# Attention and two mixtures of experts on one core: batch 0's attention in one segment, weight conversion spread, the second stage's first operands made earlier

## Chip, cores and metric

The kernel runs on one core of a Trainium2 chip. The metric is the device time of one execution in microseconds (us), smaller being better. Three runs of the kernel before took 1521.54, 1523.45 and 1525.31 us (median 1523.45).

## What is computed

Three stages, each fed by the one before. All results must have float32 accuracy.

```
attention:  4 batches, 8 heads, 576 tokens, 64 per head; block-causal mask in blocks of 64;
            softmax with row maximum; out = attn @ v         -> x (2304 tokens x 512)
first MoE:  x = (sigmoid(x @ w_gate) * (x @ w_val)) @ w_out  (512 -> 1536 -> 512)
second MoE: p = probs / (sum(probs) + 1e-9)
            out = sum over 4 experts e of p[:, e] * (relu(x @ w1[e]) @ w2[e])  (512 -> 1024 -> 512)
```

`w_gate`, `w_val` and `w_out` arrive as 64-bit floats.

## The kernel before

**Number format.** Large products are done as three fast matmuls on float32r pairs: each operand is split into a high and a low part (one copy and one subtraction, `split_sb` L101, `split3` L732). The left layers of both MoEs use a seven-product Winograd form (products 1, 5, 2, 6, 7, 4, 3), so that sums of operand blocks are made beforehand (`winograd_left` L577, `sums` L814).

**Attention** (`attn_items` L127). Work goes by pairs of heads, four pairs per batch. A pair's queries are five tiles t = 0 to 4 (the last has 64 tokens, with both heads in one tile). Per tile: scores into a PSUM bank (`s_mm` L269), mask by memset, row maximum on VectorE, exp on ScalarE with its sum, normalisation on GpSimd (`norm` L330), transposes of the weights on TensorE and copies out of PSUM (`p_tr` L361), then the product with v (`pv_both` L394), which writes its result to DRAM (`xd`, L418). Batches 1 to 3 are segments "F" with split operands. Batch 0 is done natively in float32, in two segments: "A" does tiles 0 and 1 of all four pairs against the first 256 keys, "B" then does tiles 2 to 4 of all four pairs and loads and transposes q's remaining and all of k's chunks again. In A the scores rotate through five PSUM banks (`bank` L296: two `s` banks and the first MoE's `c1`, `c2`, `lo`), in B and F through the two `s` banks. A score bank is free again when its exp has read it. The tiles that F needs (`klz`, `q4`) share space with A's and B's, so they are made when batch 0's items end (`f_tiles` L935), and F items that need them before are held (`attn_next` L946).

**Conversion.** 12 blocks of gate and value weights are turned from 64 to 32 bits, summed and split (`conv_items` L514: two loads of 512 KB; bit work on VectorE with one ScalarE pass; four subtractions, and most of the splitting, on GpSimd) and written back to DRAM as 1.8 MB per block (`wcd`, L543). Every pass of the first MoE loads them again (`w1_load` L549). Raw tiles have 3 buffers.

**First MoE.** Four passes p of 576 tokens (one batch each) by 12 blocks f. `x1_prep` (L610) needs all of that batch's attention. Pass 0 also converts `w_out` (`wo_get` L556). The second layer (`l2_1` L689) of a pair of blocks is merged with the next pair's first layer.

**Order.** `_merge` (L37) interleaves two item lists by their costs. Batch 0's attention (up to place 1.05) is merged with the first NC0 = 7 conversions. The other five follow in pass 0, half a block per f (L987). Later attention is pulled in by `attn_to` (L961). A scheduler then orders each engine's instructions at compile time with a model of time. It takes the order written here as a priority, and an instruction whose tile has no free buffer waits. All DMAs are issued by SyncE (SP), in order. Each engine runs its own queue in order.

**Second MoE.** Three passes of 768 tokens by 16 blocks q of 256 columns (`l1_items` L835, `l2_items` L886), q and q+1 in a step. `x_prep` (L743) makes a pass's seven split left operands. For pass 0 its items are emitted in the first MoE's last pass (f = 5 to 9). The weights of q (`w_load` L785, `w_prep` L793) are in the pool `p2`, which is allocated when the first MoE's pool is released (L1017), so the first two blocks and the probabilities are loaded and split there, between the two MoEs (L1020 to L1031). Each block has two tiles, `w1p` (three right operands) and `w1q` (four), two buffers each.

Of the kernel before, what the change touches and what calls it, by code (L numbers as in the profile page):

```python
# [18 lines left out]
NC0 = 7  # L19
# [8 lines left out]
PTB = 3  # L28
EARLY = True
HB = 14  # L30
PRE0, PRE1 = 0.4, 0.9
# [24 lines left out]
def attention_moe_moe_kernel(  # L56
# [70 lines left out]
    def attn_items(segs):  # L127
# [3 lines left out]

# [3 lines left out]
        QTS = {"A": range(2), "B": range(2, 5), "F": range(5)}  # L135
        KTS = {"A": range(2), "B": range(5), "F": range(5)}
# [10 lines left out]
        def load(g, nm, src, c0, c1):  # L147
            _, b, pr, seg = pairs[g]
            if nat_of(g):
                if nm == "k" and seg == "A":  # L150
                    t = attn.tile([P, S], F32, tag="kl", name="kn", bufs=2)
                    t = t[:, :2 * P].rearrange("p (c h d) -> p c h d", c=2, h=2)
                elif nm == "k" and pr % 2:
# [92 lines left out]
        order = {"A": 0, "B": 0, "F": 0}  # L246
# [6 lines left out]
        def pt_late(i):  # L253
            return not nat_of(seq[i][0]) and (seq[i][2] == 4 or ring[i] % (PT_BUFS + PT2_BUFS) >= PT_BUFS)
# [14 lines left out]
        def s_mm(i):  # L269
# [26 lines left out]
            def bank():  # L296
                if seg == "A":
# [47 lines left out]
        def pt_tile(g, h):  # L345

            i = 0 if nat_of(g) else 2 * (g - first)
            x = (i + h) % PTB
# [71 lines left out]
        def prep_list(g):  # L420
            seg = pairs[g][3]
            r = [(False, 0.0, lambda: prep_alloc(g))]
            for nm, cs in (("q", QTS[seg]), ("k", KTS[seg])):
                for part in ([c for c in cs if c < 2], [c for c in cs if c >= 2]):
                    if part:
                        r.append((seg == "F" and nm == "k", 110.0 * len(part), lambda nm=nm, part=part: prep_tr(g, nm, part)))
            if seg == "F":
                r.append((True, 0.0, lambda: prep_q4(g)))
# [28 lines left out]
        def step_tr(s):  # L457
            if 0 <= s - LT < n:
                i = s - LT
                g, hs, t = seq[i]  # L460
                items.append((g, tr_late(s - LT), 110.0 * (t + 1) * len(hs), lambda: p_tr(i)))

        def step_s(s):
            if s < n:
                g, hs, t = seq[s]
                items.append((g, pt_late(s), 2 * 0.42 * P * (t + 1) * len(hs) + 10, lambda: s_mm(s)))
# [255 lines left out]
    if True:  # L722
# [20 lines left out]
        def x_prep(p):  # L743

            r = []
            d = {}

            def load(kt):
                if kt == 0:
                    d["x"] = p2r.tile([P, NKT, TP], F32, tag="xr", name="xr")  # L750
                nc.sync.dma_start(out=d["x"][:, kt], in_=x2_d[kt][:, p * TP:(p + 1) * TP])

            def a(t, k):
                return d["x"][:, k * KH:(k + 1) * KH, t * TH:(t + 1) * TH]

            def s(which):
                if which == 1:
                    d["s"] = p2r.tile([P, KH, TH], F32, tag="xsa", name="xs")
                    nc.gpsimd.tensor_tensor(out=d["s"], in0=a(1, 0), in1=a(1, 1), op=ALU.add)
                elif which == 2:  # L760
                    nc.gpsimd.tensor_tensor(out=d["s"], in0=d["s"], in1=a(0, 0), op=ALU.subtract)
                elif which == 4:
                    nc.gpsimd.tensor_tensor(out=d["s"], in0=a(0, 1), in1=d["s"], op=ALU.subtract)
                else:
                    d["s3"] = p2r.tile([P, KH, TH], F32, tag="xsb", name="xs")
                    nc.gpsimd.tensor_tensor(out=d["s3"], in0=a(0, 0), in1=a(1, 0), op=ALU.subtract)

            def part(m, src):
                t = xc[m] = p2r.tile([P, 2, KH, TH], F32R, tag=f"xc{m}", name=f"xc{m}")
                split3(t[:, 0], t[:, 1], src())  # L770

            for kt in range(NKT):
                r.append((0.0, lambda kt=kt: load(kt)))
            for f in (lambda: part(1, lambda: a(0, 0)), lambda: s(1), lambda: part(5, lambda: d["s"]),
                      lambda: part(2, lambda: a(0, 1)), lambda: s(2), lambda: part(6, lambda: d["s"]),
                      lambda: s(3), lambda: part(7, lambda: d["s3"]), lambda: part(4, lambda: a(1, 1)),
                      lambda: s(4), lambda: part(3, lambda: d["s"])):
                r.append((0.0, f))
            return r
# [3 lines left out]
        WOP = {1: ("p", 0), 2: ("p", 1), 3: ("p", 2), 5: ("q", 0), 6: ("q", 1), 7: ("q", 2), 4: ("q", 3)}  # L783

        def w_load(q):  # L785
            e, fo = q // QPE, (q % QPE) * QF
            r1 = p2.tile([P, NKT, QF], F32, tag="wr1", name="wr1", bufs=2)
            nc.sync.dma_start(out=r1, in_=w1[e, :, fo:fo + QF].rearrange("(c p) f -> p c f", p=P))
            r2 = p2.tile([P, 2, DM], F32, tag="wr2", name="wr2", bufs=2)
            nc.sync.dma_start(out=r2, in_=w2[e, fo:fo + QF, :].rearrange("(a p) d -> p a d", p=P))  # L790
            wq["r", q] = (r1, r2)

        def w_prep(q):  # L793
# [8 lines left out]

            def own():
                r1, d["r2"] = wq.pop(("r", q))
                d["r1"] = r1.rearrange("p (h k) (a f) -> p h k a f", h=2, a=2)
                t = wq[q, "p"] = p2.tile([P, 2, 3, QF], F32R, tag="w1p", name="w1p", bufs=2)
                src = r1.rearrange("p k (a f) -> p k a f", a=2)[:, :, 0, :]
                split3(t[:, 0, 0:2].rearrange("p j (k f) -> p (j k) f", f=P),
                       t[:, 1, 0:2].rearrange("p j (k f) -> p (j k) f", f=P), src)
                split3(v(t[:, 0, 2]), v(t[:, 1, 2]), b(1, 1))  # L810

            def sums(n):
                if n == 0:
                    d["t"] = p2.tile([P, 4, QF], F32, tag="wt", name="wt", bufs=2)  # L814
# [4 lines left out]
            def mixed():  # L819
                t = wq[q, "q"] = p2.tile([P, 2, 4, QF], F32R, tag="w1q", name="w1q", bufs=2)  # L820
                split3(t[:, 0], t[:, 1], d["t"])

            def second():
                t = wq[q, "2"] = p2.tile([P, 2, 2, DM], F32R, tag="w2", name="w2", bufs=3)
                split3(t[:, 0], t[:, 1], d["r2"], "a", "p")

            r.append((0.0, lambda: own()))
            r += [(0.0, lambda n=n: sums(n)) for n in range(4)]
            r.append((0.0, mixed))
            r.append((0.0, second))  # L830
            return r

# [53 lines left out]
        def l2_items(p, q0):  # L886
# [201 lines left out]
```

## Time and profile before

| | |
|---|---|
| profiled execution, its time | 1523.15 us |
| its span | 1521.4 us (1.75 us lie outside) |
| median of the three runs | 1523.45 us |
| TensorE (PE) matmul busy | 1457.4 us, 96% |
| VectorE (DVE) / ScalarE (ACT) / GpSimd (POOL) busy | 62% / 54% / 35% |
| mean granted TensorE clock | 0.97 of full |
| batch 0's attention | to 125 us |
| first MoE | about 134 to 746 us |
| second MoE | 751 to 1518 us |

An engine's busy time is the union of its instructions. Matmul ends are modelled, so a busy PE may still have gaps inside. The clock is either 2.4 GHz (1.0) or 1.2 GHz (0.5). A value in between is a mean over the stretch. A wait row names the instruction that waited and what ended its wait.

### The profile page before, as it was taken

What the parts mean: (1) busy time and instruction counts of PE and PEld (TensorE: products, weight loads), DVE (VectorE), ACT (ScalarE), POOL (GpSimd) and SP (SyncE); (2) the same over time, 40 slices, a digit from 0 to 9 for tenths busy, and PEclk for the clock granted to TensorE, in tenths of its full rate; (3) what the DMA queues carried; (4) which work ended last, traced back from release to release, by engine and by line L of the source; (5) the groups of instructions that cost most, each with busy time, mean ns of one, the idle gap of its engine ahead of it and who ended that gap; (6) DMA issues with size and microseconds to landing.
All of it is one profiled execution on the core that took longest, in us unless ns stands there. A gap on an engine that the chain in (4) does not pass through costs nothing.

```text
span 1521.4 us, 24168 instructions
## 1 busy us (share of the span) xinstructions
PE 1457.4 (96%) x8392; PEld 1272.3 (84%) x8392; DVE 939.6 (62%) x2044; ACT 821.2 (54%) x2010; POOL 534.1 (35%) x583
## 2 busy tenths in 40 slices
PE   6877999999999999999899999999999999999998
PEld 3335788888889889999788989889898998989897
DVE  5668889887665675665665445665445475454543
ACT  5558888888875565555444433444343453343431
POOL 7685556542210110110243333363322443224320
PEclk8677999999999999999999999999999999999999
DMA  8887899887646888797422221142212123122201
GB/s 231 245 267 252 296 294 289 263 291 226 181 153 209 276 281 263 256 329 261 150 70 70 83 70 56 56 155 81 70 56 68 60 81 111 56 70 69 71 28 42
DMA packets 179242, 244.89 MB, mean 161 GB/s; under 512 B 75441, under 2 KB 124593, under 8 KB 179121
## 3 DMA queue, kind: packets, MB, share of 16 engines
q1 hardware_dynamic: 179120, 243.35, 49.6%
q8 instruction: 67, 1.10, 0.3%
q14 instruction: 55, 0.44, 0.1%
HBM read 200.84 MB, written 42.47 MB: 160 GB/s over the span
## 4 chain that ended last, share of the span: by engine, by line
PE 84%; DVE 4%; DMA 3%; ACT 3%; POOL 3%; issue 2%; SPq 1%; POOLq 0%; ACTq 0%; DVEq 0%
PE c L96 35%; PE o L96 28%; PE lo L96 7%; PE s L96 4%; PE obank L96 3%; PE tbank L369 2%; PE s L282 1%; PE t L96 1%; PE tbank L197 1%; DMA raw<-in_moe_w_gate_dram 1%; POOL wt L817 1%; ACT pt L313 1%; PE tbank L388 1%; POOL pt L341 0%; DVE nm L311 0%
## 5 line engine op out<-in xcount | busy, mean ns | idle before, releaser
L96 PE MATMUL o<-w,hb 128*128 128x512 f32 x1728 | 450.0, 395 | 2.2 <-ACT hb L864 1.0
L96 PEld LDWEIGHTS o<-w,hb 128*128 128x128 f32 x1728 | 321.9, 188 | 58.3 <-ACT hb L864 1.4
L96 PE MATMUL c<-xc,w1q 128*128 128x384 f32 x1152 | 240.9, 339 | 1.7 <-ACT w1q L735 1.4
L817 POOL TENSOR_TENSOR wt<-wr 128x256 f32<-128x256 f32 x96 | 72.2, 773 | 470.3 <-DMA wr<-in_moe_w_dram 470.3
L96 PEld LDWEIGHTS c<-xc,w1q 128*128 128x128 f32 x1152 | 207.4, 188 | 16.6 <-ACT w1q L735 2.1
L865 DVE SCALAR_TENSOR_TENSOR hb<-c,hb 128x384 fp32r<-128x384 f32 x192 | 119.4, 642 | 142.4 <-ACT hb L864 142.2
L96 PE MATMUL c<-xc,w1p 128*128 128x384 f32 x864 | 188.7, 342 | 5.9 <-ACT w1p L735 5.9
L864 ACT ACTIVATE hb<-c 128x384 fp32r<-128x384 f32 x192 | 94.7, 514 | 171.1 <-PE c L96 143.3
L96 PE MATMUL lo<-g,wo 128*128 128x288 f32 x1008 | 172.6, 302 | 3.3 <-DVE x L707 1.4
L855 ACT ACTIVATE snap<-c 128x384 f32<-128x384 f32 x144 | 69.7, 491 | 195.3 <-PE c L96 189.9
L96 PEld LDWEIGHTS c<-xc,w1p 128*128 128x128 f32 x864 | 158.4, 191 | 15.1 <-ACT w1p L735 6.4
L898 DVE SCALAR_TENSOR_TENSOR acc<-o,pr_t,acc 128x512 f32<-128x512 f32 x126 | 90.7, 747 | 129.5 <-PE o L96 129.5
L96 PEld LDWEIGHTS lo<-g,wo 128*128 128x128 f32 x1008 | 145.1, 190 | 8.4 <-DVE x L707 2.8
L341 POOL TENSOR_SCALAR pt<-pt,nm 128x384 f32<-128x384 f32 (+4 forms) x140 | 93.8, 676 | 141.8 <-DVE nm L338 100.1
L738 POOL TENSOR_TENSOR w<-wr,w 128x1024 fp32r<-128x1024 f32 x48 | 119.7, 2499 | 50.7 <-ACT w L735 50.7
L862 DVE TENSOR_TENSOR c<-c,snap 128x384 f32<-128x384 f32 x144 | 75.6, 552 | 51.6 <-ACT snap L855 47.2
L96 PE MATMUL c<-xc,wa 128*128 128x288 f32 x540 | 88.1, 302 | 4.0 <-ACT xc L108 1.9
L707 DVE TENSOR_TENSOR x<-lo,x 128x288 f32<-128x288 f32 x140 | 63.4, 453 | 34.8 <-PE lo L96 34.2
L96 PE MATMUL c<-xc,wc 128*128 128x288 f32 x504 | 82.7, 299 | 1.1 <-ACT snap L647 1.0
L96 PEld LDWEIGHTS c<-xc,wa 128*128 128x128 f32 x540 | 77.1, 190 | 8.0 <-ACT xc L108 2.2
L651 DVE TENSOR_TENSOR c<-c,snap 128x288 f32<-128x288 f32 x120 | 54.4, 453 | 45.5 <-PE c L96 31.0
L647 ACT ACTIVATE snap<-c 128x288 f32<-128x288 f32 x126 | 51.4, 408 | 57.1 <-PE c L96 56.8
(139 smaller groups left out, 2507.9 us busy)
## 6 DMA issues: line engine op xcount, KB each, us to landing
wr<-in_moe_w_dram SPq DMA_DIRECT2D x96, 512.0 KB, 3.4
wa<-wcd SPq DMA_DIRECT2D x48, 512.0 KB, 4.4
wb<-wcd SPq DMA_DIRECT2D x48, 512.0 KB, 5.0
wc<-wcd SPq DMA_DIRECT2D x48, 512.0 KB, 4.5
wo<-wod SPq DMA_DIRECT2D x36, 512.0 KB, 5.5
wd<-wcd SPq DMA_DIRECT2D x48, 256.0 KB, 4.3
raw<-in_moe_w_gate_dram SPq DMA_DIRECT2D x12, 512.0 KB, 5.6
raw<-in_moe_w_val_dram SPq DMA_DIRECT2D x12, 512.0 KB, 5.6
```

The source lines that it names most:

```text
L96: ins = nc.tensor.matmul(out=out, lhsT=lhsT, rhs=rhs, start=start, stop=stop, skip_group_check=skip)
L341: nc.gpsimd.tensor_scalar(out=p, in0=p, scalar1=nm[:, 2 + x:3 + x], scalar2=1.0, op0=ALU.mult, op1=ALU.mult)
L647: nc.scalar.activation(out=t, in_=d["c1"][:, :TH1], func=AF.Copy)
L651: nc.vector.tensor_tensor(out=c, in0=d["c2"][:, :TH1], in1=d[n], op=ALU.add)
L707: nc.vector.tensor_tensor(out=x2[t, dm], in0=ps, in1=x2[t, dm], op=ALU.add)
L738: (nc.vector if eng_lo == "v" else nc.gpsimd).tensor_tensor(out=lo, in0=src, in1=hi.bitcast(F32), op=ALU.subtract)
L817: nc.gpsimd.tensor_tensor(out=v(t[:, n]), in0=x, in1=y, op=ALU.subtract)
L855: nc.scalar.activation(out=t, in_=d["c1"][:, :TH], func=AF.Copy)
L862: nc.vector.tensor_tensor(out=c, in0=d[tag][:, :TH], in1=d[n], op=ALU.add)
L864: nc.scalar.activation(out=t[:, 0], in_=c, func=AF.Relu)
L865: nc.vector.scalar_tensor_tensor(out=t[:, 1], in0=c, scalar=0.0, in1=t[:, 0].bitcast(F32), op0=ALU.max, op1=ALU.subtract)
L898: nc.vector.scalar_tensor_tensor(out=acc[tt, t], in0=ps, scalar=pr_t[:, ti, e:e + 1], in1=acc[tt, t], op0=ALU.mult, op1=ALU.add)
```

## The change

1. Batch 0 is one segment "N": per pair all five query tiles and all keys, loaded and transposed once. All its scores rotate through five banks. Its exp tiles use a ring of four (`pt` and `pt2`), tile 4 one `pt4` buffer, the transposed weights three `pTb` buffers. The F tiles are made at the start, and nothing is held any more.
2. The first 12% of batch 0's attention are emitted ahead of any conversion. NC0 is 5. The other seven blocks are spread evenly over f = 0 to 9 of pass 0.
3. `x_prep` uses `winograd_left` with tiles of 128x384 (8 loads, 8 GpSimd sums and 14 splits per pass, in place of 4, 4 and 7 of twice the size).
4. The second MoE's `w1` operands become tiles of two products each, `w1g` (a, b, c; five buffers over all blocks) and one `w1d` buffer. They, the raw `wr1`, `wt` (one buffer) and the probabilities move to the pool `p2r`, which exists once attention has ended. `x_prep(0)`, the loads and splits of blocks 0 and 1 (less the last two splits of block 1) and the probabilities are spread over f = 2 to 11 of the first MoE's last pass. `w2` is loaded and split apart (`w2_load`, `w2_prep`), its first two blocks after the first MoE.

```diff
-NC0 = 7
+NC0 = 5
+A00 = 0.12
+W1B = 5
...
-        QTS = {"A": range(2), "B": range(2, 5), "F": range(5)}
-        KTS = {"A": range(2), "B": range(5), "F": range(5)}
+        QTS = KTS = {"N": range(5), "F": range(5)}
...
             if t == 4:
-                if nat_of(g):
-                    return attn.tile([P, S], F32, tag="kl", name="pt4", bufs=2)
                 return pt2.tile([P, S], F32, tag="pt4", name="pt4")
-            if pairs[g][3] == "A":
-                if ring[i] % (PT_BUFS + 1) == PT_BUFS:
-                    return attn.tile([P, 1280], F32, tag="pTb0", name="ptx")
-            elif pt_late(i):
+            if ring[i] % (PT_BUFS + PT2_BUFS) >= PT_BUFS:
...
             def bank():
-                if seg == "A":
+                if native:
...
-            i = 0 if nat_of(g) else 2 * (g - first)
-            x = (i + h) % PTB
+            x = (2 * g + h) % PTB
...
+            def load(kk, t, h):
+                a = p2r.tile([P, TH], F32, tag="xr", name="xr", bufs=4)
+                o = p * TP + t * TH
+                nc.sync.dma_start(out=a, in_=x2_d[h * KH + kk][:, o:o + TH])
+                return a
+            return winograd_left(p2r, xc, load, TH)
...
+        def w2_load(q):
...
+        def w2_prep(q):
+            t = wq[q, "2"] = p2.tile([P, 2, 2, DM], F32R, tag="w2", name="w2", bufs=3)
+            split3(t[:, 0], t[:, 1], wq.pop(("r2", q)), "a", "p")
...
+            def pair(k, src):
+                t = wq[q, k] = p2r.tile([P, 2, 2, QF], F32R, tag="w1g", name="w1g", bufs=W1B)
+                split3(t[:, 0], t[:, 1], src)
...
+            def last():
+                t = wq[q, "d"] = p2r.tile([P, 2, 1, QF], F32R, tag="w1d", name="w1d")
+                split3(v(t[:, 0, 0]), v(t[:, 1, 0]), b(1, 1))
+            r.append((0.0, own))
+            r += [(0.0, lambda n=n: sums(n)) for n in range(2)]
+            r.append((0.0, lambda: pair("b", d["t"][:, 0:2])))
+            r += [(0.0, lambda n=n: sums(n)) for n in range(2, 4)]
+            r.append((0.0, lambda: pair("c", d["t"][:, 2:4])))
+            r.append((0.0, last))
...
-        a0 += [(queue[i][2], attn_next) for i in range(len(queue)) if place[i] < A1[0]]
+        attn_to(A00)
+        a0 = [(queue[i][2], attn_next) for i in range(pos[0], len(queue)) if place[i] < A1[0]]
...
-                pre = x_prep(0)
-                pre0 = list(pre)
+                wp = [w_prep(0), w_prep(1)]
+                pre = x_prep(0) + [(0.0, lambda: (w_load(0), w_load(1), p_prep()))] + wp[0] + wp[1][:-2]
...
-                    if p == 0 and NC0 + f // 2 < NF:
-                        c = cs[NC0 + f // 2]
-                        side += [x for _, x in (c[:len(c) // 2] if f % 2 == 0 else c[len(c) // 2:])]
-                    if p == NP1 - 1 and f >= 5:
-                        n = len(pre) * (f - 4) // 5 - len(pre) * (f - 5) // 5 if f < 10 else 0
-                        for _ in range(n):
-                            side.append(pre0.pop(0)[1])
+                    if p == 0:
+                        c = sum(cs[NC0:], [])
+                        side += [x for _, x in c[len(c) * f // (NF - 2):len(c) * (f + 1) // (NF - 2)]]
+                    if p == NP1 - 1 and f >= 2:
+                        side += [x for _, x in pre[len(pre) * (f - 2) // (NF - 2):len(pre) * (f - 1) // (NF - 2)]]
...
-        w_load(0)
-        w_load(1)
-        run(w_prep(0))
-        run(w_prep(1))
...
+        for q in (0, 1):
+            w2_load(q)
+        prev = [(0.0, lambda q=q: w2_prep(q)) for q in (0, 1)]
...
+                if (p, q0) == (0, 0):
+                    side += wp[1][-2:]
```

## Rows read from the trace of the kernel before

**Rows 1.** The page: TensorE's busy time, and its granted clock in 40 slices.
```profile
PE 1457.4 (96%) x8392; PEld 1272.3 (84%) x8392; DVE 939.6 (62%) x2044; ACT 821.2 (54%) x2010; POOL 534.1 (35%) x583
...
PEclk8677999999999999999999999999999999999999
```
**Rows 2.** Busy time by stretch: stretch, length, busy (instructions) per engine, clock, DMA, GB/s.
```profile
0.00:126.00 126.00, 95.17 (x400) 47.56 (x400) 81.86 (x213) 73.74 (x205) 93.61 (x121) 0.78 0.83 260
42.00:126.00 84.00, 66.19 (x282) 32.27 (x281) 58.47 (x145) 50.21 (x138) 65.13 (x78) 0.76 0.84 272
62.00:82.00 20.00, 16.53 (x88) 7.95 (x88) 14.48 (x37) 12.24 (x38) 18.47 (x23) 1.00 0.83 249
...
134.00:342.00 208.00, 198.69 (x1393) 168.39 (x1391) 180.45 (x503) 179.40 (x524) 111.14 (x139) 0.98 0.86 278
342.00:500.00 158.00, 156.98 (x1132) 137.15 (x1132) 101.45 (x311) 115.83 (x346) 28.25 (x51) 1.00 0.65 199
640.00:746.00 106.00, 104.73 (x782) 103.83 (x781) 64.37 (x153) 56.08 (x159) 4.13 (x2) 1.00 0.73 251
```
**Rows 3.** SP's timeline: stores of batch 0's results (xd0a from A, xd0b from B).
```profile
41.06 0.54 SPq L418 DMA_DIRECT2D xd0a<-xr  x1
...
69.30 0.45 SPq L418 DMA_DIRECT2D xd0b<-xr  x1
...
125.39 0.52 SPq L418 DMA_DIRECT2D xd0b<-xr  x1
```
**Rows 4.** Waits from 42 to 126 us: total us, times, longest.
```profile
PEld tbank L369 <- POOL pt L341: 10.2, 7, 3.7
...
PEld s L282 <- ACT pt L313: 7.4, 5, 1.9
```
**Rows 5.** Conversion: GpSimd on tile wt to 320 us; groups by line, whole run.
```profile
sum 320.00, DVE 0.00 ACT 0.00 POOL 92.34; mean DVE 0.00 ACT 0.00 POOL 46.17
...
L110 POOL TENSOR_TENSOR wd<-raw,wd 128x256 fp32r<-128x256 f32 x12 | 9.9, 829 | 6.2 <-ACT wd L108 6.2
...
L489 DVE SCALAR_TENSOR_TENSOR raw<-raw 128x512 int32<-128x512 int32 x36 | 28.2, 782 | 0.3
L487 DVE SCALAR_TENSOR_TENSOR raw<-raw 128x512 int32<-128x512 int32 x36 | 28.1, 781 | 1.2 <-ACT raw L485 0.8
...
L486 DVE TENSOR_SCALAR raw<-raw 128x512 int32<-128x512 int32 x36 | 18.1, 503 | 11.7 <-DMA raw<-in_moe_w_gate_dram 10.5 <-DMA raw<-in_moe_w_out_dram 0.6 <-POOL wb L110 0.6
```
**Rows 6.** DMA from 134 to 342 us; SP's stores of converted blocks (a block's wd).
```profile
DMA packets 46141, 57.85 MB, mean 278 GB/s; under 512 B 27170, under 2 KB 34338, under 8 KB 46115
...
107.99 0.73 SPq L543 DMA_DIRECT2D wcd<-wd  x1
...
L543 SPq DMA_DIRECT2D wcd<-wd x12: 319/329/732, 18.1 to 305.5; - x12
```
**Rows 7.** VectorE groups by line, first from 134 to 342, then 342 to 500 us.
```profile
L651 DVE TENSOR_TENSOR c<-c,snap 128x288 f32<-128x288 f32 x36 | 16.2, 449 | 3.5 <-PE c L96 2.6 <-ACT snap L647 0.4
...
L661 DVE SCALAR_TENSOR_TENSOR r<-t,r 128x288 f32<-128x288 f32 x24 | 14.7, 611 | 0.9 <-ACT t L660 0.8
...
L651 DVE TENSOR_TENSOR c<-c,snap 128x288 f32<-128x288 f32 x33 | 15.0, 455 | 17.0 <-PE c L96 10.8 <-ACT snap L647 6.0
L661 DVE SCALAR_TENSOR_TENSOR r<-t,r 128x288 f32<-128x288 f32 x22 | 11.0, 502 | 3.6 <-ACT t L660 3.5
```
**Rows 8.** Between the MoEs (timeline); then second MoE and its middle pass by stretch.
```profile
746.43 0.41 SPq L788 DMA_DIRECT2D wr<-in_moe_w_dram  x1
...
751.24 6.13 PE L96 MATMUL c<-xc,w1p 128*128 128x384 f32 x18 [5.95 <-ACT w1p L735]
...
751.20:1517.50 766.30, 762.36 (x3744) 682.10 (x3744) 412.86 (x644) 308.19 (x541) 273.59 (x246) 1.00 0.22 73
1004.54:1256.96 252.42, 252.42 (x1250) 226.66 (x1249) 138.87 (x216) 104.74 (x183) 94.30 (x84) 1.00 0.24 79
```
**Rows 9.** Busy time by stretch: where the early x_prep items sit.
```profile
526.00:540.00 14.00, 11.50 (x68) 10.45 (x67) 8.25 (x17) 7.14 (x18) 1.81 (x1) 0.84 0.95 342
```

More of the change, by code (lines that the diff above doesn't have):

```diff
@@ L149, in load @@
             if nat_of(g):
[L150 to L153, printed above, removed]
+                if nm == "k" and pr % 2:
                     t = attn.tile([P, 5 * P], F32, tag="tk", name="kn", bufs=3)
@@ L425, in prep_list @@
                     if part:
-                        r.append((seg == "F" and nm == "k", 110.0 * len(part), lambda nm=nm, part=part: prep_tr(g, nm, part)))
+                        r.append((False, 110.0 * len(part), lambda nm=nm, part=part: prep_tr(g, nm, part)))
             if seg == "F":
-                r.append((True, 0.0, lambda: prep_q4(g)))
+                r.append((False, 0.0, lambda: prep_q4(g)))
             return [(g, *x) for x in r]
@@ L460, in step_tr @@
                 g, hs, t = seq[i]
-                items.append((g, tr_late(s - LT), 110.0 * (t + 1) * len(hs), lambda: p_tr(i)))
+                items.append((g, False, 110.0 * (t + 1) * len(hs), lambda: p_tr(i)))
         def step_s(s):
@@ L465, in step_s @@
                 g, hs, t = seq[s]
-                items.append((g, pt_late(s), 2 * 0.42 * P * (t + 1) * len(hs) + 10, lambda: s_mm(s)))
+                items.append((g, False, 2 * 0.42 * P * (t + 1) * len(hs) + 10, lambda: s_mm(s)))
         def step_norm(s):
@@ L743, in x_prep @@
         def x_prep(p):
[L745 to L778, printed above, removed]
@@ L817, in sums, with p_prep @@
                 nc.gpsimd.tensor_tensor(out=v(t[:, n]), in0=x, in1=y, op=ALU.subtract)
[L819 to L830, printed above, removed]
-            return r
+            def last():
[7 more added lines that the diff above has]
+            r.append((0.0, last))
+            return r
+        prs = {}
+        def p_prep():
+            pr_t = prs["t"] = p2r.tile([P, NTT, E], F32, name="pr_t")
+            ps_t = p2r.tile([P, NTT], F32, name="ps_t")
+            nc.sync.dma_start(out=pr_t, in_=probs.rearrange("(t p) e -> p t e", p=P))
+            nc.vector.tensor_reduce(out=ps_t, in_=pr_t, axis=AX.X, op=ALU.add)
+            nc.vector.tensor_scalar(out=ps_t, in0=ps_t, scalar1=1e-9, scalar2=None, op0=ALU.add)
+            nc.vector.reciprocal(out=ps_t, in_=ps_t)
+            for e in range(E):
+                nc.vector.tensor_tensor(out=pr_t[:, :, e], in0=pr_t[:, :, e], in1=ps_t, op=ALU.mult)
         hb = {}
@@ L921, in l2_items @@
             return r
-        a0 = [it[2:] for it in attn_items([(0, "A")])]
-        queue = attn_items([(0, "B"), (1, "F"), (2, "F"), (3, "F")])
+        queue = attn_items([(0, "N"), (1, "F"), (2, "F"), (3, "F")])
         ends = [max(i for i, it in enumerate(queue) if it[0] == x) for x in range(4)]
@@ L932, in attention_moe_moe_kernel @@
         pos = [0]
-        held = []
-        def f_tiles():
-            for x in range(3):
-                t = (attn if x < 2 else pt2).tile([P, S], F32R, tag="kl" if x < 2 else "kl2", name=f"klz{x}", bufs=2 if x < 2 else 1)
-                nc.gpsimd.memset(t[64:128].bitcast(F32), 0.0)
-                klz.append(t)
-            for x in range(2):
-                q4.append(pt2.tile([P, P], F32R, name=f"q4{x}"))
-                nc.gpsimd.tensor_scalar(out=q4[x], in0=ident, scalar1=0.0, scalar2=0.0, op0=ALU.mult, op1=ALU.mult)
-        def attn_next():
-            x, late, _, fn = queue[pos[0]]
-            if pos[0] > ends[0] and not klz:
-                f_tiles()
-                while held:
-                    held.pop(0)()
-            if not klz and x > 0 and (late or held):
-                held.append(fn)
-            else:
-                fn()
+        for x in range(3):
+            t = (attn if x < 2 else pt2).tile([P, S], F32R, tag="kl" if x < 2 else "kl2", name=f"klz{x}", bufs=2 if x < 2 else 1)
+            nc.gpsimd.memset(t[64:128].bitcast(F32), 0.0)
+            klz.append(t)
+        for x in range(2):
+            q4.append(pt2.tile([P, P], F32R, name=f"q4{x}"))
+            nc.gpsimd.tensor_scalar(out=q4[x], in0=ident, scalar1=0.0, scalar2=0.0, op0=ALU.mult, op1=ALU.mult)
+        def attn_next():
+            queue[pos[0]][3]()
             pos[0] += 1
```

48 lines of the change are left out of this document (17 added, 31 removed).

## Prediction

> **What bounds the kernel now.** I read the page first. TensorE is busy 1457.4 of 1521.4 us, and its clock is below full only in the first five slices, about 190 us [rows 1]. Then the busy time by stretch. After 134 us there is little to win on TensorE: 198.69 of 208 us, 156.98 of 158 and 104.73 of 106 [rows 2]; the second MoE's middle pass is full, 252.42 of 252.42 [rows 8]. What is lost lies in two places. Ahead of 126 us TensorE is busy 95.17 us at a mean clock of 0.78, so 95.17 x 0.78 = 74 us of work at 2.4 GHz take 126 us [rows 2]. Between the MoEs TensorE stands 5.95 us until the first split weights come [rows 8]. All else on TensorE is fixed work. A saving ahead of 126 us therefore moves the end by as much, unless the next stage gives it back. The sum is made on the profiled execution, 1523.15 us with a span of 1521.4; the median, 1523.45, is 0.3 above.
>
> **Part 1, batch 0 in one segment.** Segment A is through at 41 us, and B's stores then come 69.30 to 125.39 us, (125.39 - 69.30) / 3 = 18.7 us per pair [rows 3]. From 42 to 126 TensorE does 66.19 x 0.76 = 50 us of work at 2.4 GHz in 84: 18 us are idle and 16 go to the 1.2 GHz level [rows 2]. B has two score banks, and a score waits until an exp has freed one: 7.4 us are seen ahead of score loads, beside 10.2 us in which transposes wait for GpSimd's normalisation [rows 4]. Five banks let scores run ahead, so the first wait goes and TensorE gets denser, for which I expect the clock to stay up as it does from 62 to 82 us (1.00) [rows 2]. GpSimd is late next. A conversion block costs it 92.34 / 12 + 0.83 = 8.5 us [rows 5]; two blocks fewer are 17 us, which leaves 65.13 - 17 = 48 us in this stretch, and at the share of its densest 20 us (18.47) these need 48 / 0.92 = 52 us [rows 2]. TensorE's 50 us at nine tenths are 56. I take 56 in place of 84: **-28 us**. Ends: -52, TensorE never waiting (126 - 74); and +10, if the normalisation wait of [rows 4] doubles because tile 4 has one buffer and one queue holds all tiles. I take a value nearer the gain since both engines' rows give 52 to 56. The transposes and loads that A and B did twice (24 DMA issues of about half a us on SP) go too; taken at nothing, since SP is not what pairs wait for.
>
> Conversion begun later costs nothing by itself. Blocks come (107.99 - 18.1) / 6 = 15 us apart [rows 6], so five need 75 us, inside the 97 that remain; pass 0 needs only block 0 to begin. If that cover were missing, one block's 15 us would show.
>
> **Part 2, two more blocks in pass 0.** GpSimd gets 17 us more on 111.14, VectorE 2 x 2 x (0.782 + 0.781 + 0.503) = 8.3 us more on 180.45 of 208 [rows 2, 5], SP a dozen issues, DMA 2 x 2.9 = 5.8 MB. DMA is busy 0.86 at 278 GB/s, so 323 GB/s is full, and 57.85 + 5.8 MB need 197 us of the 208 [rows 2, 6]: it fits, closely. VectorE also gets slower beside a busy GpSimd: L661, both inputs in SBUF, takes 611 ns where GpSimd is busy 111.14 of 208 us, and 502 where it is busy 28.25 of 158; L651, one input in PSUM, takes 449 and 455 [rows 2, 7]. That is 22% for 0.35 more of GpSimd; 17 / 208 = 0.08 more are 5%, at most 9 us of VectorE's 180; I take half. VectorE then stands at 193 of 208, its free time falls from 27.6 to 15, and TensorE's idle time there, 9.3 us, would at most grow in proportion to 17. Attention pulled ahead from batch 2 can fall back to the next stretch, where VectorE is busy 101.45 of 158 [rows 2]. So **+5 us**. Ends: 0, all deferred (work is added, which excludes a gain), and +17, both blocks' whole GpSimd time. What is queued behind these GpSimd operations is batch 1's normalisation, and the transposes wait for that.
>
> The Trainium skill (GPSIMD Engine Reference, Specifications) says that GpSimd shares its SBUF interfaces with VectorE and contends with VectorE instructions that have two SBUF inputs. That speaks against this move, and the trace agrees with it. By a sum that leaves the rule out, this part would be +1 instead of +5.
>
> **Part 3, between the MoEs.** The weights are requested at 746.43 and the first product starts at 751.24, after 5.95 us [rows 8]. From there 3744 matmuls take 766.3 us, where three passes like the middle one take 757.3 [rows 8]: 9 us over, at the start (that first row has 18 products in 6.13 us, 0.34 each) and at the kernel's end, where the last step has no next one to merge with. I leave 2 to the end: 5.95 + 7 = 13 recoverable. After the change weights, x and probabilities are ready, so products follow directly; 2.5 us I leave for PSUM and SBUF handed over from the first pool. **-10.5 us**, ends -15 and -5. The moved splits (per block some 3 us each on ScalarE, VectorE and GpSimd) lie beside a pass in which VectorE has 64.37, ScalarE 56.08 and GpSimd 4.13 us in 106 [rows 2]; without that cover they would cost 6. Only `w2` is still loaded there, and it is needed a step later.
>
> **Parts 4 and 5.** The smaller `x_prep` adds seven ScalarE and VectorE instructions per pass, in a pass where ScalarE is busy 104.74 of 252.42 [rows 8]: nothing. `x_prep(0)` already runs ahead of its place, at 526 to 540 us, and TensorE is then busy 11.50 of 14 us at 0.84, losing 14 - 9.7 = 4 us [rows 9]; its eight loads may fall better or worse on SP's queue, which x2's stores and the weight loads share: 0, ends -4 and +4. Five `w1g` buffers and one `w1d` mean that a split waits until the block before has used its tile; products of the next block come behind that, with GpSimd busy 94.30 of 252.42 [rows 8] there is room: 0, end +8 (one late product of 0.34 us in each of 24 steps).
>
> **Sum:** 1523.15 - 28 + 5 - 10.5 = 1489.7, given as **1490 us**.
>
> **Rivals.** A difference under 0.3% (4.6 us) counts as the same.
> - *GpSimd, not banks, paces batch 0.* For: 10.2 us of waits for it against 7.4 for the banks [rows 4], and 18.47 of 20 us busy [rows 2]. Against: 65.13 of 84 over the whole stretch. Then 10 of the 17 us taken off GpSimd are won: 1523 - 10 + 5 - 10.5 = 1508.
> - *All engines pack.* Against: the exp, normalise, transpose chain is long. -42 in part 1, 0 in part 2, -13 in part 3: 1468.
> - *The seam stays*, because the new pool's space comes late, or its splits are put late by the scheduler. Against: x_prep's items, in the same pool, ran 100 us ahead of their place [rows 9]. 1523 - 28 + 5 = 1500.
> - *Pass 0 gives back what part 1 wins:* -10 + 17 - 10.5, 1520, the same.
> - *Slower: conversion sets pass 0's end.* In pass 0 blocks now come (305.5 - 108) / 5 = 39.5 us apart [rows 6]. At that pace seven need 276 us; if pass 0 starts at 105 (8 us behind the last store, as now), that ends at 381, 39 us behind the end of the stretch in [rows 2], 342. This decides once a block takes over (342 - 105) / 7 = 34 us. TensorE would fill half with attention of batches 2 and 3: +19 - 10.5, 1532. Against: the 39.5 us are the pace at which the items were emitted, half a block per f; ahead of it blocks took 15.
>
> **Numbers.** Chances: forecast 0.58 (its own range 1478 to 1504), GpSimd-paced 0.16, packed 0.08, seam stays 0.05, same 0.06, slower 0.07. Faster is 0.58 + 0.16 + 0.08 + 0.05 = 0.87. The range 1470 to 1517 leaves out most of the packed case, the same and the slower one, 0.2 in all.
>
> **What would show it.** Part 1: batch 0's last store near 97 us, the clock at 0.9 or more from 42 us on, no wait of score loads for exp to speak of. Part 2: TensorE at 94% or more in pass 0, L661 near 640 ns, the last converted block stored ahead of f = 11's load. Part 3: no idle over 1 us between the MoEs, and 759 to 761 us from the first product of the second MoE to the last. The forecast is wrong if batch 0's last store stays beyond 112 us, or if pass 0 grows by over 12 us.

## The result, and the profile after

The changed kernel takes **1501.11 us** (median of 4 runs, 1499.21 to 1502.30) where the kernel before took 1522.49 beside it (4 runs, 1520.00 to 1525.31): ratio 0.9858, 95% interval 0.9836 to 0.9879, or 21.6 us. The forecast was 1490, with 1470 to 1517 as its range. The profiled execution took 1501.91 us, span 1499.8; the sum was made against 1523.15, so 33.5 us were forecast and 21.2 are seen.

The page, TensorE's busy time and its clock, against [rows 1]:
```profile
PE 1441.3 (96%) x8384; PEld 1266.8 (84%) x8384; DVE 980.0 (65%) x2113; ACT 839.0 (56%) x2075; POOL 552.1 (37%) x595
...
PEclk8877999999999999999999999999999999999999
```
The clock still stands at 7 or 8 tenths in the first four slices. Now busy time by stretch, as in [rows 2] and [rows 8]:
```profile
0.00:126.00 126.00, 103.46 (x504) 59.29 (x505) 91.26 (x257) 86.98 (x252) 88.42 (x123) 0.81 0.78 240
...
134.00:342.00 208.00, 193.15 (x1309) 161.44 (x1310) 183.58 (x478) 171.62 (x491) 117.72 (x145) 0.96 0.82 266
342.00:500.00 158.00, 153.51 (x1105) 136.14 (x1104) 106.68 (x307) 113.79 (x336) 34.03 (x53) 1.00 0.76 242
...
741.90:1496.10 754.20, 751.92 (x3746) 677.68 (x3744) 438.94 (x694) 323.76 (x598) 286.36 (x246) 1.00 0.23 75
```
Ahead of 126 us TensorE gets through 504 matmuls instead of 400. From 134 to 342 it is *emptier* than before, 193.15 us against 198.69, and so is the stretch behind, 153.51 against 156.98. The second MoE is 12.1 us shorter, 754.20 against 766.30. SP's stores of batch 0, against [rows 3], with first and last start:
```profile
L402 SPq DMA_DIRECT2D xd0a<-xr x4: 339/398/584, 26.8 to 86.6; - x4
L402 SPq DMA_DIRECT2D xd0b<-xr x4: 320/545/553, 41.5 to 104.5; - x4
```
The last comes at 104.5 us, 20.9 earlier. The waits on TensorE in two stretches, 42 to 105 us (against [rows 4]) and then 220 to 342 (total us, times, longest):
```profile
PEld tbank L353 <- POOL pt L330: 3.0, 3, 1.3
PEld s L98 <- ACT pt L302: 2.5, 3, 1.3
PEld s L271 <- ACT pt L302: 2.3, 2, 1.5
...
PEld lo L98 <- DVE x L691: 7.3, 9, 2.1
...
PE lo L98 <- DVE x L691: 4.9, 5, 2.0
```
The waits of batch 0 shrank. A new one stands in pass 0, where the kernel before has none: the output product `lo` waits for VectorE to add the one before it to `x` (L691), which itself takes only 0.45 us; the rest of the wait is VectorE's queue. VectorE's gate operation (L661 before), 134 to 342 us, against [rows 7]:
```profile
L645 DVE SCALAR_TENSOR_TENSOR r<-t,r 128x288 f32<-128x288 f32 x22 | 14.2, 647 | 0.2
```
647 ns; the forecast said near 640. Between the MoEs, against [rows 8]:
```profile
741.14 0.96 PE L98 MATMUL o<-g,wo 128*128 128x288 f32 x6
741.94 3.33 PE L98 MATMUL c<-xc,w1g 128*128 128x384 f32 x18
```
No gap. The sum of the two traces: the second MoE begins at 741.94 instead of 751.24 (9.3 us, of which 5.95 are the gap) and lasts 12.1 less: 5.6 in its first step (156 products, 36.29 and then 30.64 us) and 6.4 in the other 23. So of 20.9 us won in batch 0, about **3.4** are left when the second MoE begins.

Where did they go? I counted the matmuls of each shape that are still to come before the second MoE and priced them by their spacing where the trace of before is dense at full clock (140 ns for a first-MoE product, 109 for a 128-column transpose). The difference to before is TensorE's lead in work, good to about 2 us:

| at us | changed | seven ahead | two banks | part 2 only |
|---|---|---|---|---|
| 126 | 13.8 | 11.8 | 3.0 | 3.6 |
| 180 | 18.1 | 19.5 | 5.0 | 8.8 |
| 260 | 13.4 | 16.3 | 1.2 | 7.9 |
| 342 | 3.2 | 8.8 | -8.4 | -0.6 |
| 381 | 1.0 | 7.6 | -12.2 | -0.7 |
| 690 | 3.5 | 8.5 | -15.2 | -0.8 |

The last three columns are runs told below. The lead is lost between 180 and 381 us, while pass 0 of the first MoE, the last conversions and the attention of batches 1 and 2 run together.

### The profile page after: what moved, and what is told of

Read it like the earlier page. It is cut to its first block, busy times and chain, and to the rows that moved or that the text cites. A ratio compares the mean times of both kernels' runs of the same rounds, so it can differ in the third digit from the quotient of the medians.

```text
span 1499.8 us, 24221 instructions
## 1 busy us (share of the span) xinstructions
PE 1441.3 (96%) x8384; PEld 1266.8 (84%) x8384; DVE 980.0 (65%) x2113; ACT 839.0 (56%) x2075; POOL 552.1 (37%) x595
## 4 chain that ended last, share of the span: by engine, by line
PE 80%; DVE 9%; ACT 4%; DMA 3%; issue 2%; SPq 1%; POOL 1%; DVEq 0%; ACTq 0%; POOLq 0%
PE c L98 34%; PE o L98 28%; PE lo L98 7%; PE s L98 4%; PE obank L98 3%; PE tbank L353 2%; PE t L98 1%; DVE nm L300 1%; DVE x L691 1%; DMA wr<-in_moe_w_dram 1%; DVE raw L471 1%; DMA raw<-in_moe_w_gate_dram 1%; ACT pt L302 1%; DVE g L112 1%; PE tbank L194 1%
## 5 line engine op out<-in xcount | busy, mean ns | idle before, releaser
L98 PE MATMUL o<-w,hb 128*128 128x512 f32 x1728 | 434.3, 392 | 1.4 <-ACT hb L840 1.0
L98 PE MATMUL c<-xc,w1g 128*128 128x384 f32 x1728 | 341.2, 338 | 0.9 <-ACT snap L831 0.9
L98 PEld LDWEIGHTS c<-xc,w1g 128*128 128x128 f32 x1728 | 308.9, 188 | 18.2 <-ACT snap L831 1.7
L783 POOL TENSOR_TENSOR wt<-wr 128x256 f32<-128x256 f32 x96 | 90.3, 960 | 492.5 <-DMA wr<-in_moe_w_dram 404.1
L841 DVE SCALAR_TENSOR_TENSOR hb<-c,hb 128x384 fp32r<-128x384 f32 x192 | 138.6, 734 | 61.8 <-ACT hb L840 61.5
L330 POOL TENSOR_SCALAR pt<-pt,nm 128x128 f32<-128x128 f32 (+2 forms) x144 | 94.6, 663 | 128.8 <-DVE nm L327 67.5
L722 POOL TENSOR_TENSOR w<-wr,w 128x1024 fp32r<-128x1024 f32 x48 | 116.1, 2434 | 31.5 <-ACT w L719 31.0
L719 ACT ACTIVATE w1g<-wt 128x512 fp32r<-128x512 f32 x96 | 60.4, 629 | 77.3 <-PE c L98 46.4
L722 DVE TENSOR_TENSOR w1g<-wt,w1g 128x512 fp32r<-128x512 f32 x96 | 71.9, 752 | 43.3 <-ACT w1g L719 43.0
L722 DVE TENSOR_TENSOR w1g<-wr,w1g 128x512 fp32r<-128x512 f32 x48 | 36.6, 763 | 82.9 <-ACT w1g L719 79.2
L691 DVE TENSOR_TENSOR x<-lo,x 128x288 f32<-128x288 f32 x140 | 63.4, 453 | 29.9 <-PE lo L98 29.1
```

Source lines behind the costliest of these rows:

```text
L98: ins = nc.tensor.matmul(out=out, lhsT=lhsT, rhs=rhs, start=start, stop=stop, skip_group_check=skip)
L330: nc.gpsimd.tensor_scalar(out=p, in0=p, scalar1=nm[:, 2 + x:3 + x], scalar2=1.0, op0=ALU.mult, op1=ALU.mult)
L691: nc.vector.tensor_tensor(out=x2[t, dm], in0=ps, in1=x2[t, dm], op=ALU.add)
L719: nc.scalar.activation(out=hi, in_=src, func=AF.Copy)
L722: (nc.vector if eng_lo == "v" else nc.gpsimd).tensor_tensor(out=lo, in0=src, in1=hi.bitcast(F32), op=ALU.subtract)
L783: nc.gpsimd.tensor_tensor(out=v(t[:, n]), in0=x, in1=y, op=ALU.subtract)
```

## Experiments

Theory T: in pass 0 VectorE's work sets the end, and TensorE's lead shrinks to what VectorE has done ahead. Microseconds of a run are taken by its ratio to the kernel before on its own chip, times 1523. By the intervals, a difference of under some 5 us between two runs is not clear of noise. In the diffs, "+" is the experiment.

**Halves.** Parts 1 and 2 alone, in the kernel before:
```
 (batch 0 in one segment; NC0 = 5, spread)
-w_prep, x_prep of the changed kernel
+w_prep, x_prep of the kernel before, after moe1.release()
```


> The kernel before with parts 1 and 2 only (batch 0 in one segment, five blocks ahead); the second MoE is prepared as before. Theory T (VectorE in pass 0 gives the prologue's gain back): batch 0's last store at 104 to 105 us, pass 0's results as late as in the changed kernel (361 to 381 us), the whole 1517 to 1521 us, 2 to 5 below before. Rival R (the hoisted preparation of the second MoE in pass 3 is what ate the gain): without it the prologue's 14 to 21 us stay, 1502 to 1508 us.

Measured: 1519.32, ratio 0.9967 (0.9955 to 0.9978), -5.0 us; last store 104.2, pass 0's results 360.5 to 380. T's numbers hold, R falls: the second MoE is prepared as before here, and the lead is lost all the same, at the same place. The other half:
```
-NC0 = 5, one segment
+NC0 = 7, segments A and B (as before)
```


> The kernel before with parts 3 to 5 only (second MoE's first operands beside pass 3, its tiles in smaller groups); attention and conversion as before. Theory T: this is where the measured gain sits, so 1502 to 1507 us, with no gap between the MoEs and a step of the second MoE at 31.3 us instead of 31.5. Rival R (parts help each other: the earlier end of attention makes the room): under half of it, 1512 us or more.

Measured: 1508.12, ratio 0.9892 (0.9875 to 0.9908), -16.4 us. There is no gap, and the halves add up, 5.0 + 16.4 = 21.4. The median is 1 us above T's 1507 (1506.6 by its ratio); in its profiled run, the slowest of its four, the first MoE ends 5 us later than before (750.40 against 745.3 ahead of the gap), with a clock of 0.72 up to 105 us instead of 0.79.

**One segment without the later conversion, and the reverse.**
```
-NC0 = 5
+NC0 = 7
```


> The changed kernel with seven conversion blocks ahead of pass 0 again (five in it). Theory T (one segment is worth something by itself, and the two moved blocks are only moved: what GpSimd and VectorE save ahead of pass 0 they pay in it): batch 0's last store near 113 us, pass 0's TensorE fuller (at least 38.5 of 40 us from 220 to 340), the whole within 4 us of the changed kernel, 1497 to 1505. Rival R1 (fewer blocks ahead is the whole gain of the prologue): last store 120 us or later and the whole 1505 us or more. Rival R2 (the moved blocks cost much more in pass 0 than they save, as 17 us against 8): 1490 to 1496.

Measured: 1496.66, ratio 0.9827 (0.9804 to 0.9850), -26.3, 4.7 us better than the changed kernel, at the edge of the two intervals: between T's 1497 and R2's 1496. The moved blocks seem to cost some us more in pass 0 than they saved. From 220 to 342 us TensorE is busy 114.54 us, 37.6 of 40 where T wanted 38.5. Its stores:
```profile
L402 SPq DMA_DIRECT2D xd0b<-xr x4: 319/436/1107, 41.6 to 102.4; - x4
```
With two more blocks ahead batch 0 ends at 102.4, no later than with five (104.5). R1 falls, and with it my sum for part 1, in which 17 us off GpSimd made half of the gain. I had looked for the last store near 113; it was GpSimd that I, again, took for the limit.
```
 (kernel before, segments A and B; the first 12% of attention not drawn ahead)
-NC0 = 7
+NC0 = 5, spread
```


> The kernel before with part 2 only: batch 0 stays in two segments, five blocks ahead, seven in pass 0. Theory T (moved work is paid again in pass 0): batch 0's last store some 5 to 10 us earlier, pass 0 longer by as much, the whole 1519 to 1526 us. Rival R1 (part 2 is the prologue's gain): last store near 105 and the whole 1510 to 1518. Rival R2 (costs more than it saves): 1528 or more.

Measured: 1523.70, ratio 0.9999 (0.9986 to 1.0013). The last store comes at 114.9, 10.5 us earlier, and TensorE leads by 8.8 us at 180; at 381 it is back at -0.7. T holds for the whole: moved work is paid again. With two segments, then, two blocks fewer do bring the store forward; with one segment and five banks they did not.

**The banks.**
```
-                if native:
+                if False:
                     nbank[0] += 1
```


> The changed kernel with two score banks for batch 0 instead of five, still one segment. Theory B (the banks made the prologue shorter): batch 0's last store 8 us or more later than 104.5. Rival S (one segment made it, by work of the pairs that runs together with the conversion from the start): within 3 us of 104.5. For the whole, theory T (pass 0 takes back what the prologue wins): under half of what the last store moves.

Measured: 1521.16, ratio 0.9974 (0.9961 to 0.9988), 17.7 us above the changed kernel. Its stores, and its first 126 us:
```profile
L402 SPq DMA_DIRECT2D xd0b<-xr x4: 320/540/545, 50.5 to 123.9; - x4
```
```profile
0.00:126.00 126.00, 100.39 (x411) 50.55 (x411) 72.84 (x205) 70.89 (x200) 74.08 (x102) 0.78 0.70 220
```
Theory B holds: in one segment the banks are worth 19.4 us of batch 0. One segment alone wins nothing: with two banks it ends at 123.9, and two segments with the same five blocks, of which A has five banks, ended at 114.9. T's "under half" is wrong: the whole moved by 17.7 of 19.4. Look at VectorE: 72.84 us of work by 126 us, against 91.26 (ScalarE 70.89 against 86.98, GpSimd 74.08 against 88.42). What the prologue, the time up to here, does not do on VectorE, pass 0 must. So the end of batch 0 is the wrong thing to watch; VectorE's work by then is a better one. All kernels with it, second MoE taken off (16.4 us where it has the changed one):

| kernel | last store, us | VectorE busy to 180 us | matmuls to 180 | TensorE's lead at 180, at 381 | whole, us |
|---|---|---|---|---|---|
| before | 125.4 | 127.0 | 679 | 0, 0 | 0 |
| part 2 only | 114.9 | 125.8 | 741 | 8.8, -0.7 | -0.2 |
| parts 1, 2 | 104.2 | 137.4 | 816 | 18.1, 0.8 | -5.0 |
| seven ahead | 102.4 | 142.3 | 820 | 19.5, 7.6 | -9.9 |
| two banks | 123.9 | 120.0 | 709 | 5.0, -12.2 | +12.4 |
| nine ahead | 101.2 | 141.2 | 726 | 5.5, 2.8 | -5.5 |

Up to seven blocks the whole follows VectorE's column, not the store's and not TensorE's. Steps of 2 or 3 us in this column mean nothing: the second half alone, whose first MoE is that of before, has 124.4. Two rows of it, before and then seven ahead:
```profile
0.00:180.00 180.00, 142.16 (x679) 84.04 (x681) 127.02 (x343) 121.39 (x345) 123.00 (x163) 0.81 0.82 255
```
```profile
0.00:180.00 180.00, 147.85 (x820) 95.60 (x822) 142.31 (x390) 137.00 (x399) 129.87 (x170) 0.88 0.84 262
```
The table by itself does not single out VectorE: ScalarE's busy time to 180 us puts the five kernels in the same order (118.6, 124.0, 121.4, 133.5, 137.0 from two banks to seven ahead, with part 2 only and before level), and before it is as full from 134 to 342 us (179.40 against 180.45 of 208). Against ScalarE: the changed kernel has it at 171.62 there, less than before, while VectorE rises to 183.58, and with VectorE relieved (told below) it goes back up to 179.09. And the wait of `lo` for VectorE, 7.3 and 4.9 us in the changed kernel, is down to 0.9 and 0.3 with seven ahead.

**Nine ahead.**
```
-NC0 = 5
+NC0 = 9
```


> The changed kernel with nine conversion blocks ahead of pass 0 and three in it. Theory T (VectorE's work sets the end of pass 0, and ahead of 126 us VectorE has room: busy 91 of 126 us with five blocks, 96 with seven): two more blocks ahead move about 8 us of VectorE's work there; the whole 3 to 8 us below the run with seven, 1489 to 1494 where the kernel before takes 1522 to 1524. Rival G (GpSimd, busy 102 of 126 us with seven, is full and stretches batch 0 by the 17 us that it gets): batch 0's last store at 112 us or later, the whole at or above the run with seven.

Measured: 1502.83 (three runs at 1502.8 to 1503.8, one at 1495.4), ratio 0.9856 (0.9829 to 0.9882), 4.4 us above seven ahead, not clear of noise. T's number is missed; of G, the price is right and the store is not (101.2). The blocks now run on to 137.6 us, beside batch 1, and there TensorE does less with GpSimd fuller, 126 to 180 us, nine ahead and then seven:
```profile
126.00:180.00 54.00, 42.57 (x243) 31.26 (x243) 44.30 (x117) 41.00 (x118) 38.55 (x52) 0.81 0.84 281
```
```profile
126.00:180.00 54.00, 49.10 (x335) 39.44 (x335) 46.30 (x128) 48.14 (x144) 27.40 (x38) 1.00 0.97 319
```
Pass 0's first product, too, comes 36 us later, nine ahead and then seven:
```profile
165.16 3.08 PE L98 MATMUL c<-xc,wa 128*128 128x288 f32 x12
```
```profile
129.15 1.75 PE L98 MATMUL c<-xc,wa 128*128 128x288 f32 x12
```
Until then TensorE has only batch 1's attention. Its longest waits from 126 to 180 us are for ScalarE's exp (2.8 us) and for a GpSimd split (2.4), so GpSimd is not shown as the cause. VectorE's head start helps only if TensorE has one too.

**VectorE or GpSimd in pass 0.** Each of the next two takes a like amount off one engine, and leaves out work that the result needs.
```
 def from_f64(bits, out=None, cut=False):    (cut = f >= NC0)
...
+    if cut:
+        return hi.bitcast(F32)
```


> The changed kernel; the seven blocks converted in pass 0 leave out the three integer operations of VectorE that make a 32-bit value (ScalarE's scaled upper word is used instead): 7 x 2 x (0.51 + 0.82 + 0.74) = 29 us off VectorE, nothing off GpSimd or the DMAs. Theory T (in pass 0 TensorE waits for VectorE's queue): pass 0's results come at least 10 us earlier (first store at 351 us or before instead of 361), the whole at 1487 to 1494 us. Rival G (GpSimd's share of the conversion paces it) and rival D (the DMAs): under 4 us, 1497 to 1502.

Measured: 1489.34, ratio 0.9764 (0.9741 to 0.9787), -35.9: 14.3 us below the changed kernel, on T's side. The first store of pass 0 comes at 355.4, 5.6 us earlier, not the 10 that I wrote: the rest of the time went into attention, and the lead at 381 is 9.6 instead of 1.0.
```
     def sums(n):
+        if f >= NC0: return
...
+    src of parts b and c: d[1], d[0]
```


> The changed kernel; the seven blocks converted in pass 0 leave out GpSimd's four sums each (the splits take the converted values themselves): 7 x 4 x 0.92 = 26 us off GpSimd, nothing off VectorE. Theory T: under 4 us, through a VectorE that is stretched less by its neighbour, 1497 to 1502. Rival G (GpSimd paces pass 0): first store of pass 0 at 351 us or before, the whole 1487 to 1494.

Measured: 1494.56, ratio 0.9800 (0.9774 to 0.9826), 8.8 us below the changed kernel. That is twice what T allowed. G's 1487 to 1494 is missed by half a us in the median and met by the ratio (1492.5). G's sign was a first store at 351 or before; pass 0's first stores, changed, less on VectorE, less on GpSimd:
```profile
360.94 0.32 SPq L694 DMA_DIRECT2D x2d<-x  x1
```
```profile
355.37 0.45 SPq L696 DMA_DIRECT2D x2d<-x  x1
```
```profile
352.05 6.62 SPq L698 DMA_DIRECT2D x2d<-x  x4
```
So GpSimd's relief brings the store forward by 8.9 us, more than VectorE's; in the whole it gives 5.5 us less, at the edge of the intervals. Both engines hold pass 0. What both runs share is that `lo` waits less for VectorE, 220 to 342 us, less on VectorE and then less on GpSimd (7.3 and 4.9 in the changed kernel):
```profile
PEld lo L98 <- DVE x L693: 3.1, 4, 1.2
...
PE lo L98 <- DVE x L693: 1.9, 3, 1.0
```
```profile
PEld lo L98 <- DVE x L695: 3.2, 4, 1.5
...
PE lo L98 <- DVE x L695: 2.3, 3, 1.3
```
The gate operation with less on GpSimd, 134 to 342 us:
```profile
L649 DVE SCALAR_TENSOR_TENSOR r<-t,r 128x288 f32<-128x288 f32 x23 | 12.1, 526 | 1.1 <-ACT t L648 0.9
```
526 ns against 647, and the difference of `g` (two SBUF inputs as well) takes 586 against 692. Over the 22 of each these are 22 x (0.12 + 0.11) = 5 us of VectorE's time, more than half of the 8.8; the third with two SBUF inputs did not get faster (L648: 609, then 640 ns), VectorE's total to 400 us fell by 3.2 us only, and that GpSimd also holds up normalisation by itself is not excluded. The Trainium skill (GPSIMD Engine Reference, Specifications) lets GpSimd and VectorE share SBUF interfaces; the two operations agree with it, the third does not. GpSimd's busy time alone does not set them either: with less on VectorE and GpSimd as busy as in the changed kernel (116.25 and 117.72 of 208 us) they take 583 and 612 ns.

**The seam** between the two MoEs.
```
-pre = x_prep(0) + [w_load(0), w_load(1), p_prep] + wp[0] + wp[1][:-2]
+pre = x_prep(0)
 moe1.release()
+w_load(0); w_load(1); p_prep(); run(wp[0]); run(wp[1][:-2])
```


> The changed kernel with the second MoE's first two weight blocks and the probabilities loaded and split after the first MoE's memory is given back; x of the second MoE stays prepared in pass 3, and the second MoE's smaller groups stay. Theory T: the gap between the MoEs comes back at 5 to 6 us, its first step is 2 to 4 us longer, later steps stay at 31.3 us: 1506 to 1511. Rival H (splitting them in pass 3 costs the first MoE as much): 1500 to 1503.

Measured: 1503.35, ratio 0.9858 (0.9836 to 0.9879), the changed kernel's own. But H isn't shown by it, since there is no gap: the second MoE begins right behind the first,
```profile
741.96 0.96 PE L98 MATMUL o<-g,wo 128*128 128x288 f32 x6
742.75 1.57 PE L98 MATMUL c<-xc,w1g 128*128 128x384 f32 x8
```
because the scheduler takes the loads and splits ahead as soon as their memory is free. The first loads of these weights, changed and then this run:
```profile
439.18 0.93 SPq L743 DMA_DIRECT2D wr<-in_moe_w_dram  x2
```
```profile
439.69 0.93 SPq L743 DMA_DIRECT2D wr<-in_moe_w_dram  x2
```
Both come right behind the last store of attention (436 us), not in the first MoE's last pass, over which the change spreads them in its text. The place in the program text decides nothing; the pool does. So the tiles were put into the late pool:
```
 (as above, and for wr1, w1g, wt, w1d:)
-p2r.tile(...)
+p2.tile(...)
```


> The changed kernel with the second MoE's first weight tiles in the pool that opens when the first MoE's memory is given back (as before), x still prepared in pass 3, smaller groups kept; the tiles of the second MoE come to lie about where they lay before. Theory T (the free space is what lets the scheduler fill the gap): a gap of 5 to 6 us between the MoEs, the first step longer by some 3 us, the whole 5 to 9 us above the changed kernel's, 1506 to 1510 where the kernel before takes 1522. Rival H (splitting the weights in pass 3 costs the first MoE as much): within 2 us of the changed kernel. For the step of the second MoE: theory G (smaller groups make it 31.3 us): 31.3 stays; rival A (where the tiles lie makes it): 31.5 comes back.

Measured: 1505.30, ratio 0.9875 (0.9855 to 0.9895), 2.6 us above the changed kernel, not clear of noise. The gap is back,
```profile
749.72 0.69 PE L98 MATMUL c<-xc,w1g 128*128 128x384 f32 x1 [6.16 <-ACT w1g L719]
```
and the first step is 3.7 us longer (34.31), yet the price is half of T's, because the second MoE's other steps became *shorter*. The step is the time between the loads of two steps on SP; before, changed, and late pool:
```profile
1097.14 16.54 SPq L788 DMA_DIRECT2D wr<-in_moe_w_dram  x2
...
1128.69 0.37 SPq L788 DMA_DIRECT2D wr<-in_moe_w_dram  x1
```
```profile
1078.36 15.42 SPq L743 DMA_DIRECT2D wr<-in_moe_w_dram  x2
...
1109.63 0.37 SPq L743 DMA_DIRECT2D wr<-in_moe_w_dram  x1
```
```profile
1086.97 15.24 SPq L743 DMA_DIRECT2D wr<-in_moe_w_dram  x2
...
1117.92 0.37 SPq L743 DMA_DIRECT2D wr<-in_moe_w_dram  x1
```
31.55, 31.27 and 30.95 us: neither G nor A, as I had put them. H has a part in it: where the changed kernel loads and splits the weights, this run leaves TensorE full, 420 to 460 us, changed and then late pool:
```profile
420.00:460.00 40.00, 38.07 (x274) 34.04 (x273) 24.04 (x59) 24.88 (x68) 8.80 (x11) 1.00 0.74 242
```
```profile
420.00:460.00 40.00, 40.00 (x297) 36.75 (x296) 20.03 (x58) 23.66 (x69) 2.03 (x3) 1.00 0.70 218
```
The other half of the question on the step:
```
+p2.tile(acc...) x6, p2.tile(hb)    (ahead of w2_load)
```


> The changed kernel with the second MoE's result and hidden tiles placed first, so that the tiles of the second weights lie 55 KB higher and the hidden tiles 33 KB lower; nothing else. Theory G (smaller groups make the second MoE's step 31.3 us): 31.3 stays, the whole within 3 us of the changed kernel. Rival A (where these tiles lie makes the 512-wide matmul 3 to 5 ns shorter): 31.5 us and the last 36 matmuls 8.6 us instead of 8.46; the whole 5 to 8 us above the changed kernel's.

Measured: 1502.38, ratio 0.9865 (0.9850 to 0.9879); step 31.27, last 36 matmuls 8.46 us. Where `w2` and the hidden tiles lie changes nothing, so A falls for these.

**A better version.** Seven ahead, and x where the late pool had it:
```
-NC0 = 5
+NC0 = 7
+p2r.tile(wr1), (w1g), (wt), (w1d)    (ahead of x_prep(0))
```


> The changed kernel with seven conversion blocks ahead, and with the second MoE's weight tiles placed ahead of its x tiles in their pool, so that x lies where it lay in the run with the late pool, whose step took 30.95 us. First MoE as in the run with seven ahead (first product of the second MoE near 738 us). Theory X (where x lies makes the step 30.95): the second MoE some 6 us shorter, the whole 1489 to 1492 where the kernel before takes 1523. Rival W (where the weight tiles lie, or something else): the step stays 31.27, the whole 1495 to 1498. Either way below both kernels.

Measured: 1493.58 (5 runs, 1488.04 to 1497.93), ratio 0.9814 (0.9790 to 0.9837), below both kernels, though its interval overlaps that of seven ahead and X's 1489 to 1492 is missed. The step is 1098.68 - 1067.66 = 31.02 us, and the second MoE takes 749.0 us against 755.5 with seven ahead, the 6 us that X named. But the weight tiles moved as well, so W is not excluded by this run alone. The first products of the second MoE, 42 in a row, changed and then this one:
```profile
741.94 7.54 PE L98 MATMUL c<-xc,w1g 128*128 128x384 f32 x42
```
```profile
733.50 7.45 PE L98 MATMUL c<-xc,w1g 128*128 128x384 f32 x42
```

## Why the prediction was right, and where it was wrong

The kernel got faster, by 21.6 us where 33 were forecast, inside the range. That it came as near is partly luck: the term for batch 0 was nearly three times too large, those for the second MoE too small.

- **Part 1, -28.** Batch 0 ended 20.9 us earlier; the whole gained 9.9 (seven ahead against the second half alone, both with seven blocks). Two steps failed. The first is "two blocks fewer are 17 us" off GpSimd as half of the gain: with seven blocks the last store is no later. With five banks it is the banks that win, which I had as the first of two causes; the blocks brought 10.5 us only where B's two banks stayed. TensorE's clock also stayed low, 0.78 from 42 to 105 us instead of 0.9. The second is "A saving ahead of 126 us therefore moves the end by as much, unless the next stage gives it back." I read that next stage from TensorE's share, 198.69 of 208 us, and said that there was little to win. The same row had VectorE at 180.45 and ScalarE at 179.40 of 208. This stage did not pass on a head start of TensorE alone.
- **Part 2, +5.** Measured 4.7 with one segment, at the edge of noise, and nothing alone. The size fits. The reason, VectorE slowed by a busier GpSimd, is half shown: the gate operation takes 647 ns where 640 were forecast, but 632 with seven ahead, where GpSimd is less busy (104.60 of 208 us) than before (111.14, 611 ns). The "+1 instead of +5" without that slowing does not come out of the other steps, which allow up to +4. And the mark that I set, TensorE at 94% in pass 0, failed (193.15 of 208 is 93%, 111.37 of 122 from 220 on is 91%), and pass 0, from its first product to its first stored result, went from 220.5 to 256 us, far over the 12 us that I named for a wrong forecast. Attention of batch 2 ended 22 us earlier in exchange, so the net loss is that of the table.
- **The rival "pass 0 gives back what part 1 wins"** had 0.06 and was the mechanism: 18 us of TensorE's lead at 180 us, 1 at 381. Its sum (1520) was too high: it had +7 for parts 1 and 2, where -5.0 are measured, and nothing in the second MoE beyond the seam. "GpSimd paces batch 0" fell with seven ahead, for five banks; with two segments the store moved by the 10 us that it named. "Conversion sets pass 0's end" named the right stage, but the last block was stored at 314 us, in time, so the blocks' pace did not set it; their work on VectorE and GpSimd counts.
- **Part 3, -10.5.** The 5.95 us of gap went, and the first step is 5.6 us shorter. Against that, the first MoE ends 4.2 us later than with parts 1 and 2 alone (741.94 against 743.76 less a gap of 6.07; that profiled run was the fastest of its eight). That leaves some -7. The step that failed is the cover: I put the moved splits beside a last pass with room, but they ran at 439 to 460 us and cost 3.4 us of lead there; with the weights in the late pool that loss is gone.
- **Parts 4 and 5, 0, ends -4 and +8.** Here a gain of over 4 was excluded without a reason. The steps of the second MoE became 0.28 us shorter, 12.1 - 5.6 = some 6.4 us in all, and it lasts 754.2 us where 759 to 761 were named. Why is open (last section). That made up for a part of what part 1 lacked.

Sum by the runs: -9.9 + 4.7 - 16.4 = -21.6, which comes out by the way the terms are taken; forecast -28 + 5 - 10.5.

## What to carry to other kernels

Before a saving in one stage is booked, read every engine of the next one, not the bottleneck alone: what arrives early waits in the queues of the other full engines (here VectorE's, with GpSimd beside it), and their backlog is what the first stage must shorten. Work moved into such a stage is paid again there; work moved out of it into a stage with room (seven blocks ahead instead of five) can win, here by 4.7 us that are at the edge of noise, and nine won no more. And where a scheduler orders the program, memory that is free earlier moves work, the line where it is written does not.

## What was not expected of the hardware

The same dense matmuls differ by a per cent or two between kernels at a granted clock of 1.00. From the starts of neighbouring groups in a whole pass of the second MoE, a 512-column one takes 230.9 ns before, 227.9 changed, 227.9 with `w2` moved and 225.1 with the late pool; a 384-column one 174.5, 174.0, 174.1 and 172.3, and 171.9 in the last kernel. In 22 in a row at the end, before and then changed:
```profile
1491.36 5.29 PE L96 MATMUL o<-w,hb 128*128 128x512 f32 x22
```
```profile
1476.39 5.20 PE L98 MATMUL o<-w,hb 128*128 128x512 f32 x22
```
The 384-column ones' 2 ns go with the place of the x tiles, some 35 KB away by the tiles' sizes: it is the same in the two runs that have them, while the weights lie in different places; that is an argument, not a test of x alone. What gives the 512-column ones theirs stays open: it isn't the place of `w2` and the hidden tiles. With some 6.4 of the 21.6 us these steps are no small part of the gain.
